# An attention-and-experts kernel on Trainium2: another order of instructions in its early part

## The chip, the core and the metric

The kernel runs on one core of one Trainium2 chip. TensorE (PE) multiplies matrices into PSUM, VectorE (DVE), ScalarE (ACT) and GpSimd (POOL) work elementwise, SyncE (SP) issues most of the DMAs. Each engine takes its own instructions in the order in which they were written and waits on semaphores for the others. The metric is the device time of one execution in microseconds.

## The reference

Two layers follow each other. The first is a linear attention with a decaying state; its output y, relaid as 3072 rows of 384, is the input x of the second, a mixture of eight experts whose gate is normalised over rows and columns eight times.

```python
for t in range(S):                       # B=4, H=8, S=768, D=48
    kt, vt, rt = (k[:, :, t], v[:, :, t], r[:, :, t])
    cur = np.einsum('bhd,bhe->bhde', u[None] * kt, vt)
    y[:, :, t] = np.einsum('bhd,bhde->bhe', rt, state + cur)
    state = w[None, :, :, None] * state + np.einsum('bhd,bhe->bhde', kt, vt)
...
logits = x @ w_gate                      # N=3072, D=384, E=8, F=1024
...
for e in range(E):
    h = np.maximum(x @ w1[e], 0.0)
    out += P[:, e:e + 1] * (h @ w2[e])
```

## The kernel before, in words

All instructions are written out by hand in one order, and every engine keeps its part of that order (the class `InOrder`, whose line 30 is therefore the line that most rows of the profile name; tiles tell them apart).

**Tables.** Up to about 19 us the kernel makes powers of the decay w (`rtab`, `ktab`), masks, and zeroed buffers, among them `hbx`. A second way through the attention, a scan for decays out of range, would leave its output in `hbx` (`xadd(t)` is tile t of it); with the given inputs these are zeros. `minus` is a negated unit matrix that only `low_w` uses.

**Rounds.** The loop `for i in range(last_round + 1)` at line 823 has a round for each of the 24 tiles of 128 rows (six of a batch element after each other), and two more. A round works on several tiles at once:

- `bonus_rk(i+1)`, `bonus_u(i+1)` on GpSimd: r times k, times u (tile `rk`). `bonus(i)`: VectorE sums it over a head (`dg`), GpSimd multiplies v by that, and from tile 4 on (`NEARLY`) adds `xadd(i)`.
- `prep(i+2)`: GpSimd makes r times the table (`rp`, two buffers), VectorE k times the table (`kp`, three buffers).
- `stage_b(i+1)`: TensorE transposes `rp` and `kp` (`prT`, `pkT`, four each), ScalarE copies them to `rT`, `kT`.
- `stage_c(i)`: 32 matmuls `pA` of `kT` and `rT`, and VectorE's two masked copies into `at`.
- `state_part(i-1)`, `scores_part(i-1)`: the 96 matmuls `py`, from the state `S` and from `at` and v. For the first four tiles `scores_part` adds `xadd` there by 16 matmuls with the unit matrix.
- `state_product(i)`: 32 matmuls of `kp` and v; `state_sum(i)`: VectorE adds the old state (the first tile of a batch element is multiplied by the decay on VectorE at once), GpSimd multiplies by the decay (`wbd`).
- `sum_x`, `bound_x` on VectorE: x of tile i-1 and a power of two for its scale (`xs`); `high_x` on ScalarE (`xsc`), `low_x` on VectorE: x as two halves in f16; a transposing DMA lays them into `hbx`.
- Loads of r, k, v for tile i+4, on SP behind that DMA.

**Weights of the first expert.** `magnitude`, `column_sums`, `scale_w`, `high_w` and `low_w` split w1 and w2 of expert 0 into two f16 halves while the rounds run. `hook(i, place, f)` hangs such a step on a place ("work", "gate", "mid", "end") in round i, and `run(i, place)` emits it there. For w1 `low_w` is four matmuls (`plo`) and two ScalarE copies; `magnitude` and `high_w` are ScalarE instructions over 1024 columns; `low_w` for w2 is one on VectorE.

**Blocks.** `work(n)` runs n blocks of expert 0: either nine matmuls `ph` (x times w1; ScalarE's relu and a VectorE instruction make the two halves in `hb`) or twelve matmuls `po` (times w2; ScalarE copies them out as `stg`). `ph` has two PSUM buffers, `po` two others. Blocks exist from round 4 on; until then `work` runs `spin(3)`, three matmuls of zeros (`pz`), as padding. `prepare()` does one of 68 steps on combinations of tokens from round 7 on: the first three of each group are rebuilds on VectorE, the others sums on GpSimd (`ws`), with f16 halves on ScalarE and VectorE (`xv`).

**After the rounds** a loop of ticks runs the blocks that are left, one a tick, beside 33 ticks' worth of steps (the gate's normalisation, the weights of the next stage); the last ten blocks are kept back for the stages. Then 14 stages for the other seven experts follow; these are TensorE's matmuls `bA`, `bB`, `bC`, `bY`, `bZ` and `po`, and take the rest of the time.

## Time and profile before

| what | value |
|---|---|
| median of three runs | 1564.3 us (1559.37 to 1564.52) |
| the profiled execution | 1560.4 us |
| its span, first to last instruction | 1558.9 us |
| its granted TensorE clock, mean | 0.993 |
| rounds 0 to 25 in it | about 19 to 263 us |
| first `bA` of the stages | 332.3 us |

A row of the profile's order of time has start, duration, engine, line, operation, result and operands, shape, how often; in brackets stands how long the engine had been idle before, and what ended that. Rows of matmuls overlap a little, since their ends are modelled: the time that a group takes is read from its start to the next one's. A row of the stretches has the span, then busy time and count for PE, PEld (weight loads), DVE, ACT and POOL, then the clock that TensorE was granted, the DMA engines' share and GB/s. Idle time costs only on an engine that others wait for.

### The profile page before, as it was taken

To read this page: it belongs to the slowest core of one execution; us is meant where nothing else is said; L and a number is where in the kernel's file an instruction comes from. 1 tells how busy PE (TensorE), PEld (TensorE's weight loads), DVE (VectorE), ACT (ScalarE), POOL (GpSimd) and SP (SyncE) were. 2 spreads that over 40 slices of the span, in tenths; PEclk is the share of its full clock that TensorE was granted. 3 is DMA by queue.
4 is the path that set the end of the run, shared out by engine and by line. 5 is a ranking of instruction groups with operands and counts; after the bars stand their busy time and mean duration, and the time that the engine had idled before them with its cause. 6 is when DMAs were issued, how large, how long until landed. Compare 5 with 4: busy or idle time off the path is not lost.

```text
span 1558.9 us, 29192 instructions
## 1 busy us (share of the span) xinstructions
PE 1520.8 (98%) x11808; PEld 853.8 (55%) x11808; DVE 1013.9 (65%) x1682; ACT 674.1 (43%) x1206; POOL 573.8 (37%) x682
## 2 busy tenths in 40 slices
PE   7879999999999999999999999999999999999999
PEld 4556666555555555555555555555555555555555
DVE  5677886957566666666666666666666656656554
ACT  4324333524445354544445454545444444535320
POOL 5458884520012434243342424242423324242200
PEclk8999999999999999999999999999999999999999
DMA  8355554121215566576766666664545455556434
GB/s 183 64 92 113 124 94 116 47 82 45 93 58 107 75 98 108 81 128 88 129 88 115 85 126 90 109 83 72 81 59 98 60 93 61 96 59 98 55 87 137
DMA packets 186858, 143.30 MB, mean 92 GB/s; under 512 B 109537, under 2 KB 180962, under 8 KB 186722
## 3 DMA queue, kind: packets, MB, share of 16 engines
q0 software_dynamic: 44928, 61.36, 32.3%
q1 hardware_dynamic: 141584, 80.07, 19.8%
q8 instruction: 92, 1.51, 0.4%
q14 instruction: 44, 0.36, 0.1%
q10 hardware_dynamic: 210, 0.00, 0.0%
HBM read 55.39 MB, written 80.23 MB: 87 GB/s over the span
## 4 chain that ended last, share of the span: by engine, by line
PE 89%; DVE 3%; POOL 2%; issue 1%; ACT 0%; DMA 0%; POOLq 0%; ACTq 0%; DVEq 0%; SPq 0%
PE po L30 47%; PE bZ L30 12%; PE bY L30 11%; PE bA L30 5%; PE bB L30 5%; PE ph L30 4%; PE bC L30 2%; PE py L30 1%; PE pA L30 1%; POOL rp L30 1%; POOL rk L30 1%; POOL ws L30 1%; PE prT L30 0%; PE pkT L30 0%; DVE hb L30 0%
## 5 line engine op out<-in xcount | busy, mean ns | idle before, releaser
L30 PE MATMUL po<-ws,hbx 128*128 128x384 f16 x3360 | 736.8, 326 | 0.0
L30 POOL DMA_DIRECT2D accd<-stg x288 | 249.7, 867 | 694.9 <-ACT stg L30 676.5
L30 PEld LDWEIGHTS <-hbx 128*128 128x128 f16 x3504 | 333.8, 98 | 293.4 <-issue 1.0
L30 PEld LDWEIGHTS <-ws 128*128 128x128 f16 x3096 | 302.6, 98 | 250.9 <-issue 9.3
L30 ACT ACTIVATE hbx<-tb 128x512 f16<-128x512 f32 x224 | 141.1, 630 | 450.0 <-DVE tb L30 450.0
L30 PE MATMUL po<-ws,hb 128*128 128x384 f16 x1248 | 323.0, 326 | 0.0
L30 DVE TENSOR_TENSOR tb<-bY,tb 128x512 f32<-128x512 f32 x168 | 116.2, 691 | 195.9 <-PE bY L30 195.7
L30 ACT ACTIVATE stg<-po,pe 128x384 f32<-128x384 f32 x312 | 179.1, 574 | 121.9 <-PE po L30 98.5
L30 PE MATMUL bZ<-xv,ws 128*128 128x512 f16 x840 | 227.0, 379 | 0.4 <-DVE tb L30 0.4
L30 PE MATMUL bY<-xv,ws 128*128 128x512 f16 x840 | 227.0, 379 | 0.0
L30 DVE TENSOR_TENSOR tb<-bZ,tb 128x512 f32<-128x512 f32 x168 | 115.6, 688 | 136.6 <-PE bZ L30 136.6
L30 PEld LDWEIGHTS <-hb 128*128 128x128 f16 x1248 | 121.3, 98 | 92.9 <-DVE hb L30 0.3
L30 POOL TENSOR_TENSOR ucb<-rawb 128x256 f32<-128x256 f32 x84 | 74.8, 941 | 123.5 <-DMA rawb<-in_moe_w_dram 123.5
L30 PE MATMUL ph<-hbx,ws 128*128 128x384 f16 x576 | 107.2, 332 | 5.2 <-DVE hb L30 4.2
L30 DVE TENSOR_TENSOR tb<-bB,tb 128x512 f32<-128x512 f32 x112 | 77.4, 691 | 48.8 <-PE bB L30 46.9
L30 DVE SCALAR_TENSOR_TENSOR hb<-tb,hbx 128x512 f16<-128x512 f32 x112 | 77.1, 689 | 24.6 <-ACT hbx L30 19.5
L30 PE MATMUL bA<-xv,ws 128*128 128x512 f16 x336 | 90.8, 379 | 0.0
L30 PE MATMUL bB<-xv,ws 128*128 128x512 f16 x336 | 90.8, 379 | 0.0
L30 DVE SCALAR_TENSOR_TENSOR hbx<-tb,hbx 128x512 f16<-128x512 f32 x112 | 77.6, 693 | 14.7 <-ACT hbx L30 10.4
L30 ACT ACTIVATE xsc<-x,xs 128x384 f16<-128x384 f32 x24 | 14.8, 615 | 109.8 <-DVE xs L30 85.8
L30 DVE SCALAR_TENSOR_TENSOR hb<-ph,hb 128x384 f16<-128x384 f32 x64 | 35.3, 552 | 40.6 <-ACT hb L30 40.1
L30 ACT COPY tb<-bZ 128x512 f32<-128x512 f32 x56 | 32.8, 585 | 65.5 <-PE bZ L30 65.5
(174 smaller groups left out, 1528.2 us busy)
## 6 DMA issues: line engine op xcount, KB each, us to landing
accd<-stg POOLq DMA_DIRECT2D x288, 192.0 KB, 3.7
rawb<-in_moe_w_dram SPq DMA_DIRECT2D x28, 768.0 KB, 7.0
e0d<-stg SPq DMA_DIRECT2D x48, 192.0 KB, 2.1
hb<-e0d SPq DMA_DIRECT2D x48, 192.0 KB, 3.7
vn<-in_v_dram SPq DMA_DIRECT2D x24, 192.0 KB, 4.8
accd<-stg SPq DMA_DIRECT2D x24, 192.0 KB, 1.8
accd<-hb POOLq DMA_DIRECT2D x24, 192.0 KB, 4.7
rawb<-accd SPq DMA_DIRECT2D x24, 192.0 KB, 2.5
```

Source lines behind the costliest of these rows:

```text
L30: return lambda *a, **k: self.tc.keep_in_program_order(f(*a, **k))
```

## The change

The round is emitted in another order, and some work goes elsewhere.

- `prep` is cut in two. `prep_r(i+2)` (GpSimd) moves from behind the state's decay to the third place in GpSimd's round. `prep_k(i+2)` (VectorE) moves from behind `bound_x` to ahead of `sum_x`.
- `bonus` is cut in two: `bonus_sum(i+1)` (VectorE) now ends the round before, `bonus_v(i)` stays with GpSimd and adds `xadd` for all tiles; the 16 matmuls for the first four tiles are gone.
- `stage_b(i+1)` moves from the head of round i to behind `low_x` and, from round 4 on, behind one block.
- The first `work(1, i > 4)`, with a spin set in rounds 0 to 4, becomes `work(1)` for i > 3 at that place; the second runs two blocks from round 6, not 9.
- The weight steps hang on other places: `high_w` and `low_w` of w1 are spread over rounds 1 to 3, one or two of them to a place. `minus` is made after the first tile's transposes.

```diff
-    def prep(tt):
-        ld_ = loads[tt]
-        G.tensor_tensor(rp_[tt % 2][:, :, :D], ld_["r"], rt4, op=ALU.mult)
-        V.tensor_tensor(kp_[tt % 3][:, :, :D], ld_["k"], kt4, op=ALU.mult)
...
+    def prep_r(tt):
+        G.tensor_tensor(rp_[tt % 2][:, :, :D], loads[tt]["r"], rt4, op=ALU.mult)
+
+    def prep_k(tt):
+        V.tensor_tensor(kp_[tt % 3][:, :, :D], loads[tt]["k"], kt4, op=ALU.mult)
...
-        if tt >= NEARLY:
-            aq = av.rearrange("p h d -> p (h d)")
-            G.tensor_tensor(aq, aq, xadd(tt), op=ALU.add)
+        aq = av.rearrange("p h d -> p (h d)")
+        G.tensor_tensor(aq, aq, xadd(tt), op=ALU.add)
...
-        if early:
-            xa = xadd(tt).rearrange("p (a g d) -> p g a d", g=2, d=D)
-            for g in range(2):
-                for q in range(0, P, QP):
-                    T.matmul(
-                        pys[g][q : q + QP], ident[:, q : q + QP], xa[:, g],
-                        start=False, stop=True, skip_group_check=True,
-                    )
...
-    for c in range(KC):
-        hook(1, "end", high_w, 0, c)
+    hook(1, "end", high_w, 0, 0)
     hook(2, "work", low_w, 0, 0)
-    hook(2, "gate", low_w, 0, 1)
-    hook(3, "work", low_w, 0, 2)
+    hook(2, "work", high_w, 0, 1)
+    hook(2, "end", high_w, 0, 2)
+    hook(3, "work", low_w, 0, 1)
+    hook(3, "end", low_w, 0, 2)
...
-        if i + 1 < NTT and i:
-            stage_b(i + 1)
-        run(i, "work")
-        work(1, i > 4)
         if 1 < i + 1 < NTT:
             bonus_rk(i + 1)
         if i + 1 < NTT:
             bonus_u(i + 1)
+        if i + 2 < NTT:
+            prep_r(i + 2)
         if i < NTT:
-            bonus(i)
+            bonus_v(i)
             stage_c(i)
...
-        if i == 0:
-            stage_b(1)
+        if i + 2 < NTT:
+            prep_k(i + 2)
         if 1 <= i <= NTT:
             sum_x(i - 1)
...
-        if i + 2 < NTT:
-            prep(i + 2)
-        if 1 <= i <= NTT:
-            low_x(i - 1)
...
+        if i + 1 < NTT:
+            bonus_sum(i + 1)
         run(i, "gate")
...
+        if i > 3:
+            work(1)
+        if 1 <= i <= NTT:
+            low_x(i - 1)
+        if i + 1 < NTT:
+            stage_b(i + 1)
...
+        run(i, "work")
...
-        work(2 if i > 8 else 1, i > 3)
+        work(2 if i > 5 else 1, i > 3)
         run(i, "end")
```

GpSimd around the r product of tile 4: before from the end of round 2 into round 3, now round 2 from its start. In the names `rk_3` is tile 3's r times k, `rp0` and `rp1` are the r products for TensorE's transposes, `S2` is a state; the last number of a name only tells buffers apart. Before:

```order
L30 TENSOR_TENSOR S2_178<-S2_178,wbd_165 128x192
L30 TENSOR_TENSOR rp0_169<-rn_4_400,rtab_281 128x8x48
L30 TENSOR_TENSOR rk_4_748<-rn_4_400,kn_4_402 128x384
L30 TENSOR_TENSOR rk_4_748<-rk_4_748,ub_122 128x384
L30 TENSOR_TENSOR rk_3_587<-vn_3_267,dg_3_751 128x384
L30 TENSOR_TENSOR S0_176<-S0_176,wbd_165 128x192
```

Now:

```order
L30 TENSOR_TENSOR rk_3_547<-hb3_73 128x384
L30 TENSOR_TENSOR rk_3_547<-rk_3_547,ub_121 128x384
L30 TENSOR_TENSOR rp0_168<-rn_4_399,rtab_280 128x8x48
L30 TENSOR_TENSOR rk_2_413<-vn_2_264,dg_2_503 128x384
L30 TENSOR_TENSOR rk_2_413<-rk_2_413,hbx_72 128x384
L30 TENSOR_TENSOR S2_177<-S2_177,wbd_164 128x192
```

The r product of tile 4 stood behind the decay of `S2`; now it stands three instructions ahead of it, and the add of `hbx` for an early tile is new.

ScalarE around tile 3's transposes, rounds 2 and 3 before:

```order
L30 COPY rT_3_566<-prT_3_561 128x512
L30 COPY kT_3_573<-pkT_3_568 128x512
L30 CAST ws1_75<-plo_0_0_575 128x512
L30 CAST ws1_75<-plo_0_1_579 128x512
L30 ACTIVATE xsc_1_698<-x_1_687,xs_1_694 128x384
```

Now:

```order
L30 ACTIVATE ws1_75<-ws0_74,sw_0_313 128x1024
L30 ACTIVATE xsc_1_651<-x_1_640,xs_1_647 128x384
L30 COPY rT_3_662<-prT_3_657 128x512
L30 COPY kT_3_669<-pkT_3_664 128x512
L30 CAST ws1_75<-plo_0_0_677 128x512
L30 CAST ws1_75<-plo_0_1_681 128x512
```

The copies of tile 3's transposes stood a place ahead of x of tile 1 (`xsc_1`) and now stand behind it.

TensorE from tile 3's transposes to the next `pA`, round 2 before, with a spin set (`pz`) on both sides:

```order
L30 MATMUL prT_3_561<-ident_84,rp1_170 128x128 x4
L30 MATMUL pkT_3_568<-ident_84,kp0_171 128x128 x4
L30 MATMUL plo_0_0_575<-ws0_74,scaled_316 128x512
L30 LDWEIGHTS minus_112
L30 MATMUL plo_0_0_575<-ws1_75,minus_112 128x512
L30 MATMUL plo_0_1_579<-ws0_74,scaled_316 128x512
L30 LDWEIGHTS minus_112
L30 MATMUL plo_0_1_579<-ws1_75,minus_112 128x512
L30 LDWEIGHTS zeros_108
L30 MATMUL pz_583<-zeros_108 128x512
```

Now:

```order
L30 MATMUL py_1_0_573<-vn_2_264,kp2_172 32x48 x16
L30 MATMUL prT_3_657<-ident_84,rp1_169 128x128 x4
L30 MATMUL pkT_3_664<-ident_84,kp0_170 128x128 x4
L30 MATMUL plo_0_0_677<-ws0_74,scaled_315 128x512
L30 LDWEIGHTS minus_112
L30 MATMUL plo_0_0_677<-ws1_75,minus_112 128x512
L30 MATMUL plo_0_1_681<-ws0_74,scaled_315 128x512
L30 LDWEIGHTS minus_112
L30 MATMUL plo_0_1_681<-ws1_75,minus_112 128x512
L30 LDWEIGHTS zeros_108
L30 MATMUL pz_686<-zeros_108 128x512
```

The rows are alike, but before they headed round 2, ahead of `pA` of tile 2 (the `pA` behind the padding); now they end it, behind tile 2's products, and the `pA` behind the padding is that of tile 3.

## The prediction

> **What bounds the kernel now.** I read the page's shares first, then a table of stretches cut at the start of each round's pA, then the waits in total, then TensorE's rows in order of time.

> ```profile
> span 1558.9 us, 29192 instructions
> PE 1520.8 (98%) x11808; PEld 853.8 (55%) x11808; DVE 1013.9 (65%) x1682; ACT 674.1 (43%) x1206; POOL 573.8 (37%) x682
> ```

> TensorE is busy in all but 38.1 us. The stretches say where those lie (columns: span, then busy time of PE, PEld, DVE, ACT, POOL, granted clock, DMA share, GB/s):

> ```profile
> 19.20:31.40 12.20, 10.71 (x245) 7.43 (x244) 7.66 (x16) 5.50 (x8) 6.47 (x8) 1.00 0.91 221
> 31.40:39.60 8.20, 5.25 (x15) 1.99 (x13) 3.39 (x8) 5.09 (x8) 2.71 (x3) 0.79 0.54 96
> 39.60:50.00 10.40, 10.22 (x203) 6.37 (x202) 5.94 (x12) 4.01 (x8) 4.80 (x5) 1.00 0.12 23
> 50.00:59.30 9.30, 7.29 (x191) 5.26 (x190) 6.00 (x12) 3.84 (x6) 4.68 (x5) 0.83 0.39 73
> 59.30:70.30 11.00, 9.17 (x211) 6.55 (x210) 7.00 (x17) 2.23 (x5) 5.11 (x6) 0.99 0.53 85
> 70.30:83.40 13.10, 8.71 (x156) 5.30 (x155) 7.60 (x16) 6.02 (x10) 5.25 (x5) 0.87 0.58 105
> 83.40:92.30 8.90, 7.37 (x189) 5.29 (x188) 7.71 (x18) 2.28 (x6) 4.94 (x5) 1.00 0.09 17
> 92.30:103.00 10.70, 7.90 (x167) 5.06 (x166) 10.60 (x20) 3.30 (x8) 3.36 (x4) 0.88 0.47 88
> 103.00:112.80 9.80, 8.45 (x205) 6.35 (x204) 6.61 (x15) 2.88 (x7) 9.21 (x11) 0.96 0.71 103
> 112.80:180.10 67.30, 62.48 (x1390) 45.62 (x1389) 52.64 (x102) 25.64 (x56) 55.87 (x62) 1.00 0.55 118
> 180.10:243.10 63.00, 60.90 (x1363) 43.30 (x1362) 49.29 (x101) 23.23 (x50) 56.36 (x61) 1.00 0.56 101
> 332.30:1558.90 1226.60, 1222.65 (x6696) 655.19 (x6693) 777.72 (x1203) 543.70 (x958) 374.40 (x455) 1.00 0.54 90
> ```

> From 332.30 on TensorE has 4 us of idle in 1227, and the change touches nothing there: whatever it does is a shift of that point. In rounds 0 to 8 (19.20 to 112.80, 93.6 us) the nine PE figures add to 75.07, so 18.5 us are idle; the missing clock there, span times (1 - clock) row by row, is 1.7 + 1.6 + 0.1 + 1.7 + 1.3 + 0.4 = 6.8 us. In rounds 9 to 22 TensorE is 93 to 97% busy, and GpSimd 83 to 89%. So the early rounds wait, and the rest works. For what they wait (total us, times, longest):

> ```profile
> PE prT L30 <- POOL rp L30: 10.1, 10, 2.8
> PE ph L30 <- DVE hb L30: 4.2, 3, 3.0
> ```

> And in place:

> ```profile
> 30.88 0.66 PE L30 MATMUL prT<-ident,rp 128*128 128x128 f32 x4 [0.65 <-POOL rp L30]
> ...
> 34.97 1.50 PE L30 MATMUL plo<-ws,scaled 128*128 128x512 f32 x2 [2.95 <-ACT scaled L30]
> ...
> 56.13 1.12 PE L30 MATMUL prT<-ident,rp 128*128 128x128 f32 x4 [2.01 <-POOL rp L30]
> 57.04 1.06 PE L30 MATMUL pkT<-ident,kp 128*128 128x128 f32 x4
> 57.90 1.49 PE L30 MATMUL pz<-zeros 128*128 128x512 f16 x3
> ...
> 80.44 3.04 PE L30 MATMUL ph<-hbx,ws 128*128 128x384 f16 x9 [2.96 <-DVE hb L30]
> ...
> 99.25 0.66 PE L30 MATMUL prT<-ident,rp 128*128 128x128 f32 x4 [2.80 <-POOL rp L30]
> ...
> 109.86 0.66 PE L30 MATMUL prT<-ident,rp 128*128 128x128 f32 x4 [1.35 <-POOL rp L30]
> ```

> The transposes head a round and wait for an r product that GpSimd makes last in the round before, behind the state's decay, which itself waits for VectorE and TensorE. After such a wait TensorE is slow for a while: nine ph matmuls at 3.04 where they take 1.63 later, the padding at 1.49 where 0.81 is usual.

> **The change, part by part.** *GpSimd's r product ahead, transposes behind a block.* The r product for tile i+2 is now third in GpSimd's round, and its transposes come in the latter half of the next round: more than half a round of cover, so I take all 10.1 us of that wait away, 8.0 in rounds 0 to 8 (five rows, of which four stand above, the first and the last among them; the fifth is 1.2) and 2.1 later (10.1 less 8.0). What is late next is below.

> *Weight steps spread.* The first low step (plo) stood between the transposes of tile 3 and pA of tile 2, waited 2.95 us for its scale, then ran at 0.79 of the clock. It now comes behind round 2's own work, so that wait goes.

> All 18.5 us of idle in rounds 0 to 8 thus belong to an order that is gone (8.0 r product, 2.95 scale, 4.2 block buffers, the rest in pieces under 0.8); I remove it whole with the 6.8 us of clock, and put the new order's waits in.

> *Padding and early matmuls.* Five of nine spin sets go, and the sixteen matmuls that added the scan tile to y, in each of four tiles:

> ```profile
> 41.84 0.83 PE L30 MATMUL py<-hbx,ident 128*32 128x192 f32 x16
> 42.49 0.35 PE L30 MATMUL py<-vn,kp 128*32 128x48 f32 x15
> ...
> 45.60 0.81 PE L30 MATMUL pz<-zeros 128*128 128x512 f16 x3
> 46.24 0.60 PE L30 MATMUL prT<-ident,rp 128*128 128x128 f32 x4
> ...
> 117.74 1.63 PE L30 MATMUL ph<-hbx,ws 128*128 128x384 f16 x9
> ```

> From start to start a set is 0.64 us and the sixteen 0.65: 5 x 0.64 + 4 x 0.65 = 5.8 us. In their place GpSimd gets four adds; it is busy 33 to 53% in the stretches up to 59.30 (the POOL column), which hides them: nothing.

> *More blocks early.* Rounds 4 and 6 to 8 hold one block more each. They are taken from the loop before stage 0, so TensorE's total stays; nothing, as long as that loop still has a block for each of its 33 ticks (35 remain).

> *The minus tile* leaves ScalarE's run ahead of the tables: about 0.2 us, left out.

> *What is late next.* In before, copies of a tile's transposes had a round to spare; now pA of tile i+1 follows them by a block or a spin set. ScalarE makes them behind xsc, which waits for VectorE's bound, and VectorE has k for tile i+2 ahead of that:

> ```profile
> 32.43 1.27 DVE L30 TENSOR_REDUCE wm<-pcs 128x1 f32<-128x512 f32 x2
> ...
> 40.79 1.37 DVE L30 COPY_PREDICATED at<-mask,pA 128x512 f32<-128x512 int32 x2 [5.87 <-PE pA L30]
> 43.53 0.62 DVE L30 TENSOR_TENSOR x<-py,rk 128x192 f32<-128x192 f32 x2 [1.37 <-PE py L30]
> ...
> 45.29 0.17 DVE L30 RECIPROCAL xs<-inv_s 128x1 f32<-128x1 f32 x1
> 45.37 1.09 DVE L30 TENSOR_TENSOR kp<-kn,ktab 128x384 f32<-128x384 f32 x1
> ...
> 78.34 1.57 DVE L30 SCALAR_TENSOR_TENSOR ws<-ws,sw,ws 128x1024 f16<-128x1024 f32 x1
> ```

> ```profile
> 45.49 0.61 ACT L30 ACTIVATE xsc<-x,xs 128x384 f16<-128x384 f32 x1 [5.54 <-DVE xs L30]
> ...
> 47.43 0.61 ACT L30 COPY kT<-pkT 128x512 f32<-128x512 f32 x1
> ```

> ```profile
> 39.65 1.10 PE L30 MATMUL pA<-rT,kT 64*64 64x128 f32 x32
> ```

> From pA's start the path is pA 1.1, at 1.37, k 1.09, x to xs 1.9 (43.53 to 45.46), xsc 0.6, two copies 1.1: about 7.1 us. TensorE's own round without blocks, by the starts of its rows, is 4.3 (pA 0.9, py and pu 1.8, transposes 0.9, spin 0.65). I walked the new order through these durations; what is left of the path when TensorE is through is an estimated wait. Round 1, where the column sums give TensorE 1.3 more: 1.5. Round 2, where plo gives it 2.2 but VectorE has the weight scale (1.27 and four small steps, 1.9) ahead of its mask: 1.9. Round 3, where the second plo waits for the first one's buffer: 1.1. Round 4, for the magnitudes and the second block's buffer: 1.5. Round 5, with a weight step of 1.57 and two blocks' low halves on VectorE: 2.1. Round 6, the same with three blocks: 1.8. Rounds 7 and 8, with the three rebuilds that fill VectorE for 10.60 of 10.70 us in the stretch from 92.30: 1.0 each. Sum 11.9, with 1.0 more for pieces too small to see: 12.9. Bounds: 6 if xsc is early everywhere, 18.5 if they are as long as the old ones.

> *Clock.* The 2.01 us wait was followed by 1.12 and 1.06 where transposes take 0.60 each, and 1.49 for 0.81: 1.65 us lost. Three of the new waits are near 2 us; bounds 0 and, if the old loss stays, 6.8; I take 3.0, nearer to two of three at 1.65. [...]

> **Sum:** 18.5 + 6.8 + 2.1 + 5.8 = 33.2 removed, 12.9 + 3.0 = 15.9 added: 17.3 us gained. The profiled execution took 1560.4 (span 1558.9 and 1.5 around it), which gives 1543.1. It lies 3.9 below the median of the runs, 1564.3, and 1.1 above their lowest; the new runs may lie likewise, so I say 1545.

> **Rivals.**
> (1) *The clock stays low.* Without five spin sets TensorE is idle a quarter of rounds 1 to 6, in bites of 1.5 to 2 us. For it: the clock of 0.83 to 0.88 in the stretches with a 2 us bite. Against: 1.00 in 83.40 to 92.30 with 1.5 us idle in pieces. Then 6.8 us of clock stay: gain about 13, and with waits at 16, 10; time 1550.
> (2) *The copies pace the later rounds too.* From round 9 a round is about 8.9 us of TensorE; the path above with a block's exit on ScalarE (0.5) and the gate's (0.3) is 7.9, a margin of 1.0. If VectorE comes to its mask 2.1 us late in each of 15 rounds, TensorE waits 1.1 in each: 16.5, the gain is gone, 1563. Against it: VectorE is busy 78% in 180 to 243, so lateness of a round is mostly made up.
> (3) *Slower.* The same place at a higher price: VectorE, now holding k ahead of x and a block's low half ahead of xsc, is late by 2.8 us or more a round, at which also the transposes stand, since they take the PSUM banks that the mask frees. It decides from 1.7 us of wait a round: 15 x 1.7 = 25.5, less 17.3 gained, 8 slower; 1572.
> (4) *Loads late.* Tile 5's loads go out behind the first transposing DMA as before, but r is wanted half a round earlier and rounds are shorter.

> ```profile
> 32.58 1.34 SPq L30 DMA_TRANSPOSE hbx<-xsc  x1
> 34.03 0.52 SPq L30 DMA_DIRECT2D rn<-in_r_dram  x1
> ```

> By the walk that load moves to about 31 and is wanted at about 36; a landing 5 us later would cost 5 in one round: 1550.

> **How the numbers follow.** My forecast, a gain of 13 to 25: 0.61. Rival 1: 0.14. Rival 4: 0.05. Rival 2, within the noise: 0.15. Rival 3: 0.05. About 0.5% (7.8 us, so 1556.5) is what a measurement of this kernel tells from no change: faster 0.61 + 0.14 + 0.05 = 0.80, same 0.15, slower 0.05. The low end takes new waits at 6 and no clock loss, 33.2 - 6 = 27.2 gained from 1564.3: 1537, rounded to 1536; the high end waits at 18.5 and clock at 6.8, 7.9 gained from 1564.3: 1556, taken as 1557; it leaves out rivals 2 and 3.

> **What would show it.** Right: no wait for rp before prT; pA of tile 9 near 104 us (112.8 now) with four blocks more done; stage 0's first bA near 315 (332.3); new waits of PE for ACT's rT or kT in rounds 1 to 6, none over 2.5 us; the same 1223 us busy behind. Wrong: rounds 9 to 22 longer than 9.4 us with waits for rT, kT or at; or a clock under 0.85 in rounds 1 to 6 throughout.

## The result

The changed kernel takes 1541.3 us, the median of three runs (1539.95 to 1542.09), against 1562.2 for the kernel before in runs beside them (1559.37 to 1564.52). A fourth run at a granted clock of 0.65 is left out. The ratio is 0.9866, with a 95% interval of 0.9838 to 0.9893: about 21 us, or 1.3%, faster. The profiled execution took 1542.1 us, 18.3 less than that of before.

The changed kernel's profile, its page's first rows:

```profile
span 1540.6 us, 29055 instructions
PE 1507.9 (98%) x11729; PEld 850.5 (55%) x11729; DVE 1005.2 (65%) x1682; ACT 672.9 (44%) x1206; POOL 580.4 (38%) x686
```

The stretches of the changed kernel, cut at pA of tiles 0, 2 to 9, 16 and 23 and at the first bA, so that the first row holds rounds 0 and 1 (columns as before: span, then busy time of PE, PEld, DVE, ACT, POOL, granted clock, DMA share, GB/s):

```profile
18.50:28.52 10.02, 8.59 (x220) 6.03 (x220) 8.29 (x17) 5.65 (x9) 9.69 (x12) 1.00 0.95 229
28.52:36.37 7.85, 6.84 (x178) 4.64 (x178) 7.38 (x19) 3.07 (x6) 5.63 (x8) 1.00 1.18 160
36.37:47.81 11.44, 9.23 (x183) 5.61 (x183) 6.47 (x13) 6.13 (x10) 8.41 (x10) 1.00 0.78 96
47.81:56.53 8.72, 8.23 (x195) 6.01 (x194) 5.75 (x13) 5.57 (x8) 4.67 (x6) 1.00 0.62 70
56.53:65.49 8.96, 6.53 (x156) 4.87 (x155) 7.82 (x21) 4.64 (x7) 5.38 (x7) 1.00 0.48 91
65.49:76.76 11.27, 8.65 (x199) 6.27 (x198) 8.59 (x17) 4.17 (x8) 7.62 (x6) 1.00 0.60 114
76.76:86.59 9.83, 8.88 (x182) 6.38 (x181) 7.97 (x20) 3.26 (x9) 0.59 (x1) 1.00 0.21 36
86.59:95.88 9.29, 9.29 (x215) 6.88 (x214) 7.46 (x16) 3.15 (x8) 7.03 (x8) 1.00 0.70 157
95.88:161.62 65.74, 61.90 (x1384) 45.42 (x1383) 49.01 (x103) 25.32 (x56) 56.44 (x61) 1.00 0.66 121
161.62:230.65 69.03, 63.65 (x1372) 45.73 (x1371) 48.40 (x102) 23.41 (x52) 60.29 (x68) 0.98 0.47 92
314.12:1540.60 1226.48, 1222.49 (x6695) 655.20 (x6693) 777.90 (x1203) 543.40 (x958) 373.69 (x455) 1.00 0.53 90
```

The work from the first bA on is the same 1226.5 us with 1222.5 busy: the whole gain lies ahead of it. In rounds 0 to 8 the eight rows add to 77.38 us with 11.1 idle, where before had 93.6 with 18.5, and the granted clock is 1.00 in all of them. pA of tile 9 starts at 95.88. But the first bA is at 314.12 and was at 332.31: part of what was gained by tile 9 went again, and in the stretch from 161.62 TensorE is idle 5.4 us at a clock of 0.98.

TensorE's waits in the changed kernel (total us, times, longest):

```profile
PE py L30 <- issue: 7.2, 6, 1.9
PE ph L30 <- DVE hb L30: 5.3, 4, 2.4
PE pA L30 <- ACT kT L30: 4.3, 6, 1.3
PE px L30 <- issue: 2.0, 1, 2.0
```

The 10.1 us of prT for rp and the 3.0 of plo for its scale are gone. New are 4.3 for ScalarE's copies ahead of pA; and "issue", time in which nothing that the profile names was missing, went from 5.3 (py and ph in before) to 9.3 with a last 0.2 ahead of prT. The largest such row of before:

```profile
PE py L30 <- issue: 5.0, 4, 1.9
```

Rows of TensorE in the changed kernel in order of time, from five places:

```profile
28.52 1.17 PE L30 MATMUL pA<-rT,kT 64*64 64x128 f32 x31 [1.30 <-ACT kT L30]
...
40.86 0.37 PE L30 MATMUL py<-vn,kp 128*32 128x48 f32 x13 [1.79 <-issue]
...
63.94 1.62 PE L30 MATMUL ph<-hbx,ws 128*128 128x384 f16 x9 [2.35 <-DVE hb L30]
...
211.41 0.46 PE L30 MATMUL py<-vn,at 128*32 128x48 f32 x24 [1.87 <-issue]
...
212.31 3.57 PE L30 MATMUL po<-ws,hb 128*128 128x384 f16 x12
```

The wait for kT in round 2 stands where the prediction put it. The longest of the early waits, 2.35 us, did not slow the nine ph matmuls behind it (1.62); the 1.87 in round 21 was followed by twelve po at 3.57 where 2.11 is usual.

### The profile page after: what moved, and what is told of

It reads as the page before. It is cut to its first block, busy times and chain, and to the rows that moved or that the text cites. A ratio compares the mean times of both kernels' runs of the same rounds, so it can differ in the third digit from the quotient of the medians.

```text
span 1540.6 us, 29055 instructions
## 1 busy us (share of the span) xinstructions
PE 1507.9 (98%) x11729; PEld 850.5 (55%) x11729; DVE 1005.2 (65%) x1682; ACT 672.9 (44%) x1206; POOL 580.4 (38%) x686
## 3 DMA queue, kind: packets, MB, share of 16 engines
q8 instruction: 92, 1.51, 0.4%
## 4 chain that ended last, share of the span: by engine, by line
PE 84%; DVE 1%; issue 1%; ACT 0%; DMA 0%; SPq 0%; ACTq 0%; DVEq 0%
PE po L30 46%; PE bZ L30 12%; PE bY L30 12%; PE bA L30 5%; PE bB L30 5%; PE ph L30 2%; PE bC L30 2%; PE py L30 0%; DVE tb L30 0%; DVE wms L30 0%; PE pA L30 0%; DVE xv L30 0%; DMA hbx<-xsc 0%; PE pc L30 0%; DVE hb L30 0%
## 5 line engine op out<-in xcount | busy, mean ns | idle before, releaser
L30 PE MATMUL po<-ws,hbx 128*128 128x384 f16 x3360 | 736.8, 326 | 0.0
L30 POOL DMA_DIRECT2D accd<-stg x288 | 249.7, 867 | 693.5 <-ACT stg L30 672.1
L30 PEld LDWEIGHTS <-hbx 128*128 128x128 f16 x3504 | 333.9, 98 | 296.7 <-issue 4.2
L30 PEld LDWEIGHTS <-ws 128*128 128x128 f16 x3096 | 301.9, 98 | 249.4 <-issue 6.7
L30 ACT ACTIVATE hbx<-tb 128x512 f16<-128x512 f32 x224 | 141.1, 630 | 449.9 <-DVE tb L30 449.9
L30 PE MATMUL po<-ws,hb 128*128 128x384 f16 x1248 | 324.4, 327 | 0.9 <-DVE hb L30 0.9
L30 DVE TENSOR_TENSOR tb<-bY,tb 128x512 f32<-128x512 f32 x168 | 116.2, 692 | 195.8 <-PE bY L30 195.6
L30 ACT ACTIVATE stg<-po,pe 128x384 f32<-128x384 f32 x312 | 179.1, 574 | 122.0 <-PE po L30 98.9
L30 PE MATMUL bZ<-xv,ws 128*128 128x512 f16 x840 | 227.0, 379 | 0.4 <-DVE tb L30 0.4
L30 PE MATMUL bY<-xv,ws 128*128 128x512 f16 x840 | 227.0, 379 | 0.0
L30 DVE TENSOR_TENSOR tb<-bZ,tb 128x512 f32<-128x512 f32 x168 | 115.6, 688 | 136.0 <-PE bZ L30 136.0
L30 PEld LDWEIGHTS <-hb 128*128 128x128 f16 x1248 | 121.8, 98 | 94.8 <-issue 1.4
L30 POOL TENSOR_TENSOR ucb<-rawb 128x256 f32<-128x256 f32 x84 | 75.8, 953 | 117.7 <-DVE hbx L30 81.2
L30 DVE TENSOR_TENSOR tb<-bB,tb 128x512 f32<-128x512 f32 x112 | 77.5, 692 | 49.1 <-PE bB L30 47.2
L30 PE MATMUL ph<-hbx,ws 128*128 128x384 f16 x576 | 104.2, 326 | 5.3 <-DVE hb L30 5.3
L30 DVE SCALAR_TENSOR_TENSOR hb<-tb,hbx 128x512 f16<-128x512 f32 x112 | 77.2, 689 | 24.6 <-ACT hbx L30 19.5
L30 PE MATMUL bA<-xv,ws 128*128 128x512 f16 x336 | 90.8, 379 | 0.0
L30 PE MATMUL bB<-xv,ws 128*128 128x512 f16 x336 | 90.8, 379 | 0.0
L30 DVE SCALAR_TENSOR_TENSOR hbx<-tb,hbx 128x512 f16<-128x512 f32 x112 | 77.5, 692 | 14.7 <-ACT hbx L30 10.4
L30 DVE SCALAR_TENSOR_TENSOR hb<-ph,hb 128x384 f16<-128x384 f32 x64 | 35.3, 555 | 50.1 <-ACT hb L30 49.6
L30 ACT COPY tb<-bZ 128x512 f32<-128x512 f32 x56 | 32.8, 585 | 65.5 <-PE bZ L30 65.5
L30 ACT ACTIVATE xsc<-x,xs 128x384 f16<-128x384 f32 x24 | 14.8, 615 | 106.1 <-issue 53.2
```

What stands on the lines that cost most here:

```text
L30: return lambda *a, **k: self.tc.keep_in_program_order(f(*a, **k))
```

## The experiments

The first round starts at up to 3.3 us different times in the profiles, so each kernel is also told by one stretch of its own profile, from pA of tile 0 to the first bA: 313.1 us before, 295.6 in the changed kernel. Ratios are to runs of the kernel before on the same chip. The last two columns say what lies in that stretch: the sum of TensorE's issue waits, and the clock lost, which is the time at a lower granted clock times the missing share.

| kernel | median us | ratio, 95% | stretch us | issue us | clock us |
|---|---|---|---|---|---|
| before | | 1 | 313.1 | 5.3 | 6.8 |
| changed | 1541.3 | 0.9866 (0.9838 to 0.9893) | 295.6 | 9.3 | 1.7 |
| e1, transposes at the head | 1551.4 | 0.9940 (0.9927 to 0.9952) | 307.0 | 3.8 | 8.5 |
| e2, r product behind the decay | 1539.0 | 0.9863 (0.9848 to 0.9877) | 294.2 | 9.1 | 0 |
| e3, weight steps as before | 1545.9 | 0.9908 (0.9893 to 0.9922) | 300.7 | 8.3 | 5.1 |
| e4, blocks as before | 1537.3 | 0.9855 (0.9840 to 0.9869) | 290.6 | 4.7 | 0 |
| e5, padding kept | 1541.3 | 0.9885 (0.9871 to 0.9900) | 294.6 | 7.2 | 0 |
| e6, k behind the bound | 1536.3 | 0.9852 (0.9837 to 0.9866) | 290.3 | 6.7 | 1.7 |
| e7, before with r ahead | 1558.2 | 0.9988 (0.9979 to 0.9996) | 311.2 | 6.0 | 10.2 |
| e8, before with transposes moved | 1548.6 | 0.9928 (0.9915 to 0.9941) | 299.2 | 5.9 | 0 |
| e9, before with r and k ahead | 1559.5 | 0.9991 (0.9982 to 1.0000) | 310.4 | 4.9 | 8.5 |
| e10, 48 more matmuls at the start | 1542.6 | 0.9882 (0.9866 to 0.9897) | 297.6 | 10.4 | 5.1 |
| e11, e4 and e6 together | 1535.7 | 0.9842 (0.9828 to 0.9855) | 291.4 | 6.1 | 1.7 |
| e12, before with two moves | 1542.7 | 0.9891 (0.9874 to 0.9907) | 295.8 | 5.2 | 3.5 |

A stretch is that of a single execution, and the lost clock in it differs between executions of the same kernel (the mean granted clock of e8's runs goes from 0.993 to 0.999), so a stretch can be some us off the median. With both columns taken off, before has 301.0, e8 293.3, e12 287.1 and the changed kernel 284.6. This is an estimate, and a rough one: e10, whose work on the path is that of the changed kernel, has 282.1, so a difference of 2.5 us in it tells nothing.

**Parts undone in the changed kernel**

```diff
+        if i + 1 < NTT and i:      # at the top of the loop
+            stage_b(i + 1)
...
-        if i + 1 < NTT:            # behind low_x
-            stage_b(i + 1)
```

> The changed kernel with its transposes put back at the head of the round (tile i+1 at the head of round i, ahead of pA of tile i); the r product stays ahead of the decay. Theory (the r product's late place was the cost; once it is ahead, the transposes can stand in either place): no wait of prT for rp, pA of tile 9 at 94 to 98 us (95.9 in the changed kernel), first bA at 311 to 317 (314.1), the 4.3 us that PE waits for ACT's kT gone. Rival A (the gain is the transposes' place, since at the head they have nothing queued between them and pA): waits in front of prT or pA of 1 us a round come back, pA of tile 9 at 101 or later, first bA at 320 or later.

The theory's numbers failed and the rival's came: pA of tile 9 at 109.3, the first bA at 323.4, the stretch 307.0, 11.3 longer, of which 6.8 is lost clock. No wait for rp to speak of returned (0.5 us), but py waited 5.3 us for at, 3.1 of it in one place, and 6.0 for the copies. Since the first block was not put back between the transposes and pA, this kernel only says that work must stand there.

```diff
-        if i + 2 < NTT:            # ahead of bonus_v
-            prep_r(i + 2)
...
+        if i + 2 < NTT:            # behind bound_x and high_x
+            prep_r(i + 2)
```

> The changed kernel with GpSimd's r product put back behind the state's decay; the transposes stay behind one block. Theory (either of the two edits alone gives the r product half a round of cover): waits of prT for rp under 2 us in total, pA of tile 9 at 95.5 to 98, first bA at 313 to 317. Rival A (the r product's place is needed by itself): prT waits for rp 5 us or more in total, first bA at 319 or later.

The theory held: the stretch is 294.2, and prT waits 0.5 us for rp. (First bA came at 310.9, 2.1 ahead of the theory's range, in a profile whose first round starts 1.8 earlier.) With the transposes behind the sums, the place of the r product is worth nothing that these runs tell.

```diff
+    for c in range(KC):
+        hook(1, "end", high_w, 0, c)
+    hook(2, "head", low_w, 0, 0)
+    hook(2, "gate", low_w, 0, 1)
+    hook(3, "head", low_w, 0, 2)
```

> The changed kernel with the steps of w1 where the kernel before has them: the three high halves at the end of round 1, the low halves at the head of round 2, behind round 2's sums and at the head of round 3. Theory (the wait of plo for its scale and the slow clock behind it are a cost of their own): a wait of about 3 us in front of plo ahead of pA of tile 2 and a granted clock under 0.9 behind it, pA of tile 9 3 to 6 us later than the changed kernel's 95.9, first bA at 317 to 320. Rival B (the early rounds have room, VectorE and ScalarE catch up): the wait is there but pA of tile 9 is within 1.5 us of 95.9 and first bA within 2 of 314.1.

The theory held: the first bA is at 318.0, and the stretch is 5.1 longer, by this wait (row of TensorE's waits in e3) and 3.4 us more of lost clock:

```profile
PE plo L30 <- ACT scaled L30: 4.0, 1, 4.0
```

The step behind it ran at 2.07 us for two matmuls that take 1.02, and pA of tile 2 came 17.7 us behind that of tile 0, where the changed kernel has 10.0. At pA of tile 9 the loss is 7.9, more than the theory's 3 to 6; part of it is made good later.

```diff
-        if i > 3:
+        if i > 4:
             work(1)
...
-        work(2 if i > 5 else 1, i > 3)
+        work(2 if i > 8 else 1, i > 3)
```

> The changed kernel with the blocks as before: none behind the sums in round 4, two a round at the second place from round 9 on, not from round 6. TensorE's total work is the same. Theory (four blocks are only moved, and hide some of the waits in rounds 4 to 8): pA of tile 9 at 89 to 93 us, first bA 1 to 4 us later than 314.1. Rival C (the four blocks fill time that is idle otherwise, so they are a good part of the gain): pA of tile 9 at 94 or later, first bA at 320 or later, 6 or more lost of the 18.2.

Both missed the end: pA of tile 9 came at 89.2, as the theory has it, but the stretch is 290.6, 5.0 shorter. TensorE's waits in e4:

```profile
PE pA L30 <- ACT kT L30: 4.9, 6, 1.6
PE ph L30 <- DVE hb L30: 4.0, 3, 2.3
PE py L30 <- issue: 3.4, 5, 1.1
...
PE ph L30 <- issue: 1.3, 2, 0.9
```

The other waits rose by 1.1 in sum; those for issue fell from 9.3 to 4.7 and the lost clock from 1.7 to 0, which together is the size of the gain. The issue waits that went lie behind pA of tile 9 (7.4 there in the changed kernel, 1.8 in e4), where the two kernels run the same blocks a round. So this run does not show that blocks in early rounds cost anything by themselves.

```diff
-        if i > 3:
-            work(1)
+        work(1, i > 3)
...
+        if early:                  # tt < 4, as in the kernel before
+            xa = xadd(tt).rearrange("p (a g d) -> p g a d", g=2, d=D)
...
```

> The changed kernel with the padding and the early matmuls back: a spin set ahead of the transposes in rounds 0 to 3, and the sixteen matmuls that add the scan tile for tiles 0 to 3 (GpSimd's add only from tile 4). Measured from pA of tile 0 to the first bA, since the start varies by 1.5 us from profile to profile: 313.1 us before, 295.6 in the changed kernel. Theory (the prediction's term: 4 x 0.64 + 4 x 0.65 = 5.2, less some 1 us of waits for kT that they fill): 299 to 301.5. Rival (they stand in time in which TensorE waits for the copies or the next pA anyway): 295 to 297.

The rival's number came, but not for its reason. At pA of tile 9 the kernel is 4.9 us behind the changed one (82.3 us from pA of tile 0, against 77.4), as the theory wants. By the first bA it is 1.0 ahead. The changed kernel has 7.4 us of issue waits after tile 9 (1.97, 0.74, 1.14, 0.19, 1.87, 1.46), this one 2.6 (1.03 and 1.55): these 4.8 us, and the 1.7 of lost clock, which this one has not, make up the 5.9 that change hands there.

```diff
-        if i + 2 < NTT:            # ahead of sum_x
-            prep_k(i + 2)
...
+        if i + 2 < NTT:            # behind bound_x and high_x
+            prep_k(i + 2)
```

> The changed kernel with VectorE's k product (tile i+2) put back behind the bound of x, so that x, its scale, ScalarE's xsc and the copies behind it come up to 1.1 us earlier in a round. From pA of tile 0 to the first bA: 295.6 in the changed kernel. Theory (VectorE makes k in a gap in which it waits for py, so its place costs nothing either way): 294 to 297. Rival D (the k product ahead of x is on the path to the copies, as the prediction's walk has it): PE's waits for kT fall from 4.3 us to under 2 and the stretch is 290 to 293.5. Rival E (behind, it delays the blocks' low halves on VectorE): waits of ph for hb rise above 5.3 and the stretch is 297.5 or longer.

Rival D: 290.3, 5.3 shorter, the median below the changed kernel's by 5. TensorE's waits in e6:

```profile
PE py L30 <- issue: 5.7, 7, 1.2
...
PE pA L30 <- ACT kT L30: 1.3, 2, 0.7
PE px L30 <- DMA hbx<-xsc: 1.2, 1, 1.2
PE px L30 <- issue: 1.1, 1, 1.1
```

The waits for kT fell from 4.3 to 1.3, which is 3.0 of the 5.3 us; those for issue fell from 9.3 to 6.7, and those for hb rose by 0.8. The k product ahead of x is on the path to the copies, as the prediction's walk had it; VectorE does not make it for nothing.

**Single parts done in the kernel before**

```diff
+        if i + 2 < NTT:            # ahead of bonus, third on GpSimd
+            prep_r(i + 2)
...
-            prep(i + 2)
+            prep_k(i + 2)
```

> The kernel before with one edit: GpSimd's r product for tile i+2 third in its round, ahead of the state's decay; all else as before, the transposes at the head with the block or padding between them and pA. From pA of tile 0 to the first bA: 313.1 us before, 295.6 in the changed kernel. Theory (the wait for rp, 8.0 us in rounds 0 to 8 and 10.1 in all, and the slow clock behind it are what this order loses): no wait of prT for rp over 0.5 us, stretch 301 to 307. Rival A (the transposes at the head only wait for the next late thing, the PSUM banks that VectorE's mask and sums free): waits in front of prT, pkT or py of 6 us or more in total in rounds 0 to 8, stretch 309 or longer.

Only 1.9 us came of it. The stretch misses the theory's by 4 and lies in the rival's range; but the wait did not go to banks, as the rival has it, but to the second product. The waits of prT and pkT for the two products fell from 11.2 to 7.8, and 3.4 us more of clock were lost. TensorE's waits in e7, and its row ahead of pA of tile 4:

```profile
PE pkT L30 <- DVE kp L30: 7.1, 7, 2.1
```

```profile
56.68 0.63 PE L30 MATMUL pkT<-ident,kp 128*128 128x128 f32 x4 [2.08 <-DVE kp L30]
```

In the kernel before prT waited 2.01 us at this place; in e7 pkT, four matmuls later, waits 2.08. Both products were late; the profile named the one that came last.

```diff
-        if i + 1 < NTT and i:
-            stage_b(i + 1)
         run(i, "work")
-        work(1, i > 4)
...
+        work(1, i > 4)             # behind the sums
...
+        if i + 1 < NTT:            # behind low_x
+            stage_b(i + 1)
```

> The kernel before with one edit: the transposes of tile i+1 and the first block (or padding) go from the head of the round to behind the sums, the block first, as in the changed kernel; the r product stays behind the decay, the weight steps where they were. From pA of tile 0 to the first bA: 313.1 us before, 295.6 in the changed kernel. Theory (the change's gain is mostly this move; with the r product put back the changed kernel kept all of its gain): waits for rp under 2 us, stretch 301 to 306. Rival (the move needs the r product ahead or the weight steps spread): 309 or longer.

The theory's direction held, and the stretch is shorter than its range: 299.2, which is 13.9 of the 17.5 us. But this execution lost no clock, where that of before lost 6.8, and it was 2.5 us faster than its kernel's median. By the medians the move is worth 11 us, of the 21 of the whole change. No wait for rp or kp is left among TensorE's. What stands instead (e8):

```profile
PE pA L30 <- ACT kT L30: 4.5, 4, 1.5
PE ph L30 <- DVE hb L30: 4.0, 3, 2.4
PE plo L30 <- ACT scaled L30: 3.2, 1, 3.2
```

The move gives both products most of a round more, and takes it from the copies, which had it to spare but for 4.5 us.

```diff
+        if i + 2 < NTT:            # third on GpSimd
+            prep_r(i + 2)
...
+        if i + 2 < NTT:            # ahead of sum_x on VectorE
+            prep_k(i + 2)
```

> The kernel before with two edits: the r product for tile i+2 third in GpSimd's round, and the k product for tile i+2 ahead of x's sums on VectorE; transposes at the head, weight steps, blocks and padding as before. From pA of tile 0 to the first bA: 313.1 us before, 311.2 with the r product ahead alone, where pkT waited 7.1 us for kp instead. Theory (the transposes wait for whichever of the two products comes last; with both ahead the wait is gone): waits of prT and pkT under 1.5 us in total, stretch 301 to 306. Rival (they then wait for a third thing, the PSUM banks or the copies): waits ahead of the transposes, pA or py of 5 us or more in rounds 1 to 8, stretch 308.5 or longer.

The theory failed and the rival's number came: 310.4, and the timed ratio, 0.9991, tells no change. TensorE's waits in e9, and the longest in its place:

```profile
PE ph L30 <- DVE hb L30: 6.0, 3, 4.8
...
PE plo L30 <- ACT scaled L30: 3.7, 1, 3.7
...
PE py L30 <- DVE at L30: 2.4, 2, 2.1
PE prT L30 <- POOL rp L30: 2.0, 1, 2.0
...
PE pkT L30 <- DVE kp L30: 1.5, 2, 1.1
```

```profile
80.24 3.04 PE L30 MATMUL ph<-hbx,ws 128*128 128x384 f16 x9 [4.78 <-DVE hb L30]
```

The transposes wait 3.5 us together (rp 2.0, kp 1.5), not 10. But TensorE then meets VectorE, which is late with its mask (2.4 us, 0.7 in before) and with a block's low half (4.8 us at a place where before waits 3.0). That the k product, 1.26 us in round 5 and now ahead of x, is what makes it late is argued from the order, not tested. To bring the producers forward moved the wait from engine to engine; to move their reader back (e8) removed it.

**What the issue waits are**

```diff
     spin(19)
+    for _ in range(48):            # while TensorE waits for wc
+        T.matmul(pz[:, :P], zeros[:, :P], zeros[:, :P], start=True, stop=True)
```

> The changed kernel with 48 more matmuls of zeros in the time before the tables, where TensorE waits 4.1 us for wc: no work on the path, only a longer stream of instructions. TensorE's waits that the trace lays to issue stand in the changed kernel, and in seven kernels so far, near matmul 82 + 127 n, and end 1.3 to 1.8 us behind a 16384-byte packet of the instruction queue. Theory F (TensorE's instructions are fetched in blocks of about 127 matmuls with their weight loads, and a block of quick small matmuls is used up before the next has come): the issue waits stand at the same counts 82 + 127 n, so 48 matmuls earlier in the program (not at px of round 9, nor at the 24 last py of round 21), and their sum changes by 1 us or more from 9.4; from pA of tile 0 to the first bA 295.6 becomes 293 to 300 by the difference. Rival G (they belong to places of the program, a transposing DMA or a form of matmul): they stay at the same tiles, at counts higher by 48, and the stretch stays within 1 us of 295.6.

Theory F. Matmuls counted up to three issue waits, in the changed kernel and then in e10 (stretches from 0; the first number with x is TensorE's count):

```profile
0.00:40.86 40.86, 30.34 (x588) 19.75 (x589) 30.93 (x59) 20.95 (x28) 31.18 (x42) 0.92 0.97 182
0.00:137.59 137.59, 116.32 (x2490) 81.49 (x2490) 102.03 (x213) 60.98 (x108) 102.25 (x115) 0.98 0.71 126
0.00:211.41 211.41, 186.22 (x4009) 132.24 (x4009) 160.20 (x333) 87.81 (x168) 161.68 (x179) 0.98 0.68 124
```

```profile
0.00:32.81 32.81, 23.91 (x462) 15.94 (x463) 23.52 (x47) 16.13 (x21) 25.80 (x36) 0.99 0.98 207
0.00:132.09 132.09, 112.44 (x2362) 78.33 (x2363) 93.54 (x198) 56.97 (x100) 93.99 (x108) 0.96 0.64 127
0.00:206.38 206.38, 182.21 (x3883) 128.86 (x3884) 151.63 (x318) 84.70 (x161) 151.96 (x169) 0.98 0.62 122
```

With a step of 126.75 from 82 these six are steps 4, 19, 31 and 3, 18, 30, to within three matmuls: e10 waits at other places of the program, at counts of the same grid. Of 92 issue waits in the rounds of all fourteen kernels, all but two (0.16 us each) stand within 7 matmuls of it. The page of the changed kernel has a queue of the kind instruction with this row:

```profile
q8 instruction: 92, 1.51, 0.4%
```

1.51 MB in 92 packets is 16.4 kB each; 11729 matmuls and as many weight loads over 92 are 127 pairs a packet. The packets' own times fit it in the two traces of before and of the changed kernel: their thirteen issue waits in the rounds end 1.26 to 1.76 us behind the end of such a packet (in the changed kernel 39.53 and 40.86, 99.04 and 100.80, 210.08 and 211.41). Of the 184 packets of both 159 take 0.9 to 1.5 us, and of the 74 that start before 260 us 53 start 0.3 to 2.5 us after TensorE has entered the block ahead. At eleven of the thirteen waits that block had been used up in 1.9 to 3.4 us; at the other two (8.9 us before the wait that ends at 49.97, 6.5 before 211.41) the packet had started late, 6.5 and 5.4 us after the block was entered. That TensorE's instructions come in such blocks, and that it waits where one is used up before the next has come, is the author's reading of these counts and times.

The time answers less clearly: the sum of issue waits is 10.4 us against 9.3, and the stretch is 2.0 longer. The clock lost is 5.1 against 1.7, and 3.4 of that stands behind one wait, the longest (slow rows up to the plo at 37.09, 1.91 where 1.02 is usual). This is TensorE at it, in round 2 of e10:

```profile
32.81 0.45 PE L30 MATMUL py<-vn,kp 128*32 128x48 f32 x9 [3.82 <-issue]
33.19 1.12 PE L30 MATMUL prT<-ident,rp 128*128 128x128 f32 x4
34.10 1.06 PE L30 MATMUL pkT<-ident,kp 128*128 128x128 f32 x4
```

**Put together**

> The changed kernel with two edits undone at once: the k product behind the bound of x (alone it took 5.3 us from the stretch from pA of tile 0 to the first bA, 295.6 in the changed kernel) and the blocks as before (alone 5.0 us). Theory (the first removes waits for ScalarE's copies, the second changes which instructions meet the late fetches, so they add up in part): stretch 284 to 289, median 1530 to 1535. Rival (both gains are the same idle time, or luck with the fetches): 289.5 to 292, median 1535.5 or more.

The edit is that of e4 and of e6. The rival came: 291.4, median 1535.7, at the edge of its range. The two gains do not add; the stretches of e4, e6 and e11 lie within 1.1 us of each other. What they share wasn't separated. e11 beats the kernel before by 1.6% (0.9828 to 0.9855); its runs (1535.37 to 1537.71) lie below all three of the changed kernel, but the intervals of the two ratios overlap.

> The kernel before with two edits alone: the transposes with the first block (or padding) behind the sums, and the weight steps of expert 0 spread as in the changed kernel. The r and k products, the number of blocks a round, the padding and the early matmuls stay as before. From pA of tile 0 to the first bA: 313.1 us before, 299.2 with the first edit alone, 295.6 in the changed kernel. Theory (these two edits are the gain; by the single undoings the weight steps are worth 5.1 and the other parts nothing or less): 290 to 296, median 1535 to 1541. Rival (the other parts, each worth nothing alone, are worth something together): 297.5 or longer, median 1544 or more.

This is e8 with the weight steps hung as in the changed kernel, and nothing else:

```diff
+    hook(1, "end", high_w, 0, 0)
+    hook(2, "work", low_w, 0, 0)
+    hook(2, "work", high_w, 0, 1)
...
-        run(i, "work")             # at the top of the loop
...
-        run(i, "mid")
+        run(i, "work")
```

The stretch is 295.8 where the changed kernel has 295.6: the theory's place, though the median is 1.7 above its range. Two edits carry the gain: 17 us by the medians, with an interval that overlaps that of the changed kernel. The r and k products ahead, the added blocks and the removed padding add up to nothing that these runs tell.

## Why the prediction was right, and where not

The time forecast, 1545, is 3.7 above the median, and the point at which it is decided came where it was put: first bA near 315, and 314.12 in the profile. Terms inside the sum were off both ways, and the other point that it named was missed: pA of tile 9 near 104, and 95.88 in the profile. The 1.9 that it put on for the median was not borne out either: the profiled execution took 1542.1 and the median is 1541.3.

- *r product ahead, transposes behind a block.* The wait is gone, as predicted, and with the clock lost behind it this is most of the gain. But the prediction laid the wait to the r product alone, and that step was wrong: the k product was nearly as late. e7 and e2 show that the r product's new place does next to nothing (1.9 us at most); the transposes' move is what removes the wait (e8: no wait for either product, 11 us by the medians).
- *Weight steps spread.* Right in kind and size: predicted 2.95 of wait and slow matmuls; 5.1 by undoing it (e3), 3.4 by adding it to e8 (e12; 5.9 by the medians).
- *Padding and early matmuls, 5.8.* Mis-sized in the end. e5 shows 4.9 by tile 9 and nothing at the first bA; the issue waits and the lost clock behind tile 9, both larger in the changed kernel, took it back. The issue waits fall on other instructions there: on steps 21 and 32 of the grid in e5, on 13, 16, 19, 24, 31 and 33 in the changed kernel.
- *More blocks early, nothing.* Not confirmed: without them the stretch is 5.0 shorter (e4). The issue waits fell by 4.6 and the lost clock by 1.7 with it, so these waits are the likely cause; that is argued from the sums, not separated from the blocks.
- *New waits, 12.9.* Idle time in rounds 0 to 8 is 11.1, of which 2.0 are issue waits. The waits for kT, the path that was walked, are only 1.7 of it (1.30 and 0.41 in rounds 2 and 3); those for the block buffers hb are 5.3, in rounds 4 to 6, with 2.35 in round 5, where 2.1 was forecast. So the sum was near and its parts were not. (In the walk, the figures given for round 2 make 2.8 - 2.2 + 1.9 = 2.5, not 1.9; measured for kT there are 1.3.) That the k product lies on the path to the copies, e6 confirms.
- *Clock, 3.0.* Failed: 1.00 in all of rounds 0 to 8, so nothing was lost there. Yet 1.87 us in round 21 was followed by slow rows (twelve po at 3.57 where 2.11 is usual). That nothing was lost early is in part luck: e10, with the same order of work, lost 1.7 us behind the like wait of 2.36 us (ph at 2.53 and pA at 1.81, where the changed kernel has 1.62 and 1.10 behind its 2.35); where in the clock's windows the 2.35 fell is in the last section. (The prediction's 0.79 for the first plo is the mean of its row: the clock was 0.5 from 35.59 to 39.00. Its cut at 31.40 is not a pA, so its first two rows are rounds 0 and 1 together; the sums stand.)
- *What the sum lacked.* At tile 9 the kernel is 16.2 us ahead with four more blocks done, some 23 in equal work at 1.5 to 2 us a block (from start to start, the ph at 63.94 takes 1.55, the po at 110.79 in before 2.04), more than the 15 of the sum. From there to the first bA about 6 were lost again. Issue waits (7.4 against 4.8 in before) are 2.6 of that and the half clock from 212.78 to 216.20 is 1.7; the rest isn't traced. The early terms took too little off, and the late loss was not in the sum at all: the two nearly cancelled. That the end came out right is luck.

The rivals: the clock did not stay low (1); rounds 9 to 22 did become longer, 9.6 us each (from 95.88 to 230.65 in 14) against the 9.4 named as a limit, but of these 4.5 us more than in before, 2.6 are issue waits and 1.7 lost clock: kT makes only 1.9 us there, in three rows, about what the waits for rp made there before (2, 3); no load held TensorE up (4).

## What to carry to other kernels

When a reader waits for two producers, the profile names only the later one: here to bring that one forward handed the wait to the other (rp 10.1 us and kp 1.1 in before, 0.7 and 7.1 in e7), while moving the reader back by part of a round removed both, at the price of 4.5 us of waits for what comes behind it (e8). Undo each part of a many-part change alone, since parts that cost (here the k product ahead) hide behind one that pays. And where TensorE runs thousands of small matmuls, count them: in e10 48 more moved the issue waits to other instructions. The issue waits sum to between 3.8 and 10.4 us in the kernels here, so a difference of a few us between two kernels can come from that; 48 matmuls alone made 1.0 in the waits and 2.0 in the stretch (e10). Before a small difference is given to an edit, take these waits and the lost clock off both sides.

## What was not expected of the hardware

The clock behind a wait does not follow from its length alone. Waits of 2.35 us (the changed kernel, at 63.94) and 2.08 (e7, at 56.68) were followed by matmuls of the usual time (ph at 1.62; pkT at 0.63 and pA at 1.10). Waits of 1.87 us (the changed kernel, at 211.41), 2.01 (before, at 56.13) and 2.06 (e9, at 58.40) were followed by slow ones (po at 3.57 for 2.11; prT at 1.12 for 0.60; 64 py at 1.51 for 0.89), and so were the longest, 3.82 in e10 (prT at 1.12) and 4.78 in e9 (ph at 3.04). The traces of before and of the changed kernel show what may differ: all changes of the granted clock in them lie whole multiples of 3.413 us apart (in the rounds of before it falls to 0.50 at 35.59, 56.07, 79.96 and 100.44 and is back at 39.00, 59.48, 83.38 and 103.85; in those of the changed kernel it falls at 212.78 and is back at 216.20). Cut into windows on that step, these are the ones around the 2.01 us of before (first two rows) and the 2.35 us of the changed kernel (last three; columns as above):

```profile
52.65:56.07 3.42, 1.48 (x47) 0.73 (x36) 2.46 (x8) 0.56 (x2) 1.53 (x3) 1.00 0.44 74
56.07:59.48 3.41, 3.35 (x15) 2.18 (x19) 2.16 (x3) 3.41 (x6) 3.27 (x4) 0.50 0.14 29
...
59.18:62.59 3.41, 2.41 (x18) 1.69 (x17) 3.27 (x11) 1.05 (x2) 1.37 (x2) 1.00 0.86 166
62.59:66.00 3.41, 2.06 (x28) 1.28 (x31) 3.14 (x6) 3.12 (x7) 3.33 (x4) 1.00 0.02 4
66.00:69.42 3.42, 3.42 (x160) 2.81 (x153) 3.42 (x9) 1.13 (x2) 1.47 (x2) 1.00 0.94 178
```

The wait of before lies in one window, which is 1.94 us idle, and the next runs at half clock. The longer one of the changed kernel is split, 1.00 and 1.35 us idle, and costs nothing. From the first round to the first bA of these two, the full-speed windows that were followed by one at half clock are five, with 2.79, 1.94, 2.48 and 2.22 us of idle in before and 1.87 in the changed kernel; no other has more than 1.79. That the idle time inside one window decides is the author's reading of these two traces; no run tested it.
